# The spectral stage's B product over 128 array lines, with Y turned by transfers inside SBUF, and one order of units over all batches

## The chip, the cores and the metric

The kernel runs on one core of a Trainium2 chip. The core has TensorE (PE, matrix products into PSUM), VectorE (DVE), ScalarE (ACT), GpSimd (POOL) and SyncE (SP, which here issues transfers only). The metric is device microseconds of one execution; lower is better. The time before is 894.48 us, the median of three runs (893.96 to 896.12).

## The reference

The input x has 8 batches of 3008 rows by 256 columns. Along the rows it goes through a real Fourier transform, is multiplied by a complex 256 x 256 weight, gets a bias, is soft-thresholded at 0.01, and is transformed back. Every row of the result goes through a two-layer network with 2048 hidden units and an ELU.

```python
X = np.fft.rfft(x, axis=1)
Yr = Xr @ w_r - Xi @ w_i + b_r
Yi = Xr @ w_i + Xi @ w_r + b_i
Yr = np.sign(Yr) * np.maximum(np.abs(Yr) - lam, 0.0)      # Yi likewise, lam = 0.01
y = np.fft.irfft(Yr + 1j * Yi, n=3008, axis=1)
h = y @ w_in                                              # 256 -> 2048
g = np.where(h > 0.0, h, np.exp(np.minimum(h, 0.0)) - 1.0)
out = g @ w_out                                           # 2048 -> 256
```

## The kernel before

**Two stages in one stream.** 3008 = 47 x 64, so each Fourier transform is done as two short ones with a re-sorting through DRAM between them. A batch's spectral work is cut into 40 *units* that PE computes: 6 units A (first short transform, 2 matmuls each), 8 units X (second short transform, 8 matmuls), 12 units M (the complex weight, by three products, 6 matmuls), 6 units B (first inverse transform, 8 matmuls) and 8 units Y (second inverse transform, 8 matmuls). After the A units the result A is stored to a DRAM tensor DA and read back re-sorted as Z; after the B units, Bz is stored to DB and read back as Bs. Y units give yT, the input of the network, in bf16.

The network runs over blocks of 512 rows; batches do not end on block borders. Each block has 8 *steps*, 376 steps in all (47 per batch). A step i does, in PE's order: two front matmul groups (L797, one per hidden slice of 128), with at most one spectral unit between them, and then the back matmuls of step i - 2 (L852, 8 matmuls in fp32r). ACT takes exponentials of the front result, POOL or DVE clamps them, DVE mixes them into gT (L832), which the back matmuls read two steps later. After the last of a block's eight steps the output is copied from PSUM to osb, one half by DVE and one by ACT (L863), and stored by SP (L870); this falls on the steps with i mod 8 = 1, called output steps below.

**What a unit costs the other engines.** Each unit's PSUM result (one tile, pool psF) is evicted before the next unit may write it: by ACT for A, X, B and Y (L126, L336). An M step is different (`unit_M`, L244): DVE adds the product K and the bias (L272, L273, or L266 and L269 where DVE adds the whole bias), POOL adds the rest of the bias (L282), clips (L283) and subtracts (L286), which gives Y; POOL also makes the difference Xd for the M unit two further on (L240). In a step without M, POOL clamps the exponentials (L820, two of 128x512); in a step with M, ACT does a variant that needs no clamp (L811, L813). The POOL work of an M is queued in `jobs` and its last part is issued in the step after.

**The B unit** (`unit_B`, L311). Y holds two M units' results (i = 0, 1); its 128 partitions are two halves (s = 0, 1) of 64, and its columns hold real and imaginary part (c = 0, 1). The inverse product sums over 64 lines and over c, so before the change it has eight matmuls of 64 lines by 256 columns, two of which accumulate into each of four results. M3 is the table of sines and cosines for it.

**The order of units** (`plan(b)`, L879) is written per batch of 47 steps: Y units of batch b, the 8 X, 12 M and 6 B of batch b + 1 with A units of batch b + 2 as filler between, then the first two Y of batch b + 1 so that they fall on steps 38 + b and 39 + b of the 47. `f0` holds the unit of a step, `f1` what is issued after it: loads of x (POOL's queue), of Z and Bs (SP's queue), the first differences. With A for a filler, Y for a Y unit and "-" for no unit, the order before (47 steps to a line, from step 0) is

```
-YY-YYXXXXXXXXYMMMMBMYMBMMBMMBMMBABAAAYYAA-----
YYXXXXXXXXYMYMMYMBMYMBMMBMAMBMMBABAAAA-YY------
YYXXXXXXXXYMYMMYMBMYMBMAMBMAMBMMBABAAA--YY-----
YYXXXXXXXXYMYMMYMBMYMBMAMBMAMBMAMBABAA---YY----
YYXXXXXXXXYMYMYMYMBMAMBMAMBMAMBMAMBABA----YY---
YYXXXXXXXXYMYMYMYMBMAMBMAMBMAMBMAMBABA-----YY--
YYXXXXXXXXYMYMYMYMBM-MBM-MBM-MBM-MB-B-------YY-
YYYYYY-----------------------------------------
```

Batch 0's units up to its second Y, and batch 1's A units, are done ahead of step 0, in the first 58 us.

Of the kernel before, what the change touches and what calls it, by code (L numbers as in the profile page):

```python
# [16 lines left out]
N2 = 64  # L17
K1 = 24
# [7 lines left out]
def kernel(  # L26
# [31 lines left out]
    wcat_s = constp.tile([P, 2, 2 * D], BF16, name="wcat_s")  # L58
# [5 lines left out]
    bias_p = constp.tile([P, 2 * D], BF16, name="bias_p")  # L64
# [16 lines left out]
    xtp = ctx.enter_context(tc.tile_pool(name="xtp", bufs=1))  # L81

# [20 lines left out]
    Bz_of = {}  # L103
    DB_of = {}
# [97 lines left out]
    def m_group(b, q, i, ps, biased=False):  # L202
        XT = XT_of[b]
        o = (2 * q + i) * P
        if biased:
            nc.tensor.matmul(ps, lhsT=busy[:, 0:P], rhs=bias_p[:], start=True, stop=False)
# [25 lines left out]
    jobs = []  # L232

# [10 lines left out]
    def unit_M(b, q, i):  # L244
# [15 lines left out]
        Y_ = Y_of[b, q]  # L260

        def done():
            two = lambda t: t.rearrange("p (c d) -> p c d", c=2)
            if b == 1 and k % 2 == 0:
                Kb = wk1.tile([P, 2 * D], F32, name="Kb", tag="Kb")
                nc.vector.tensor_tensor(  # L266
                    two(Kb[:]), kp.unsqueeze(1).to_broadcast([P, 2, D]), two(bias_bc[:]), ALU.add
                )
                nc.vector.tensor_tensor(yb[:], ps[:, 0], Kb[:], ALU.add)  # L269
# [3 lines left out]
            nc.vector.tensor_tensor(  # L273
                two(yb[:]), two(ps[:, 0]), Kb.unsqueeze(1).to_broadcast([P, 2, D]), ALU.add
            )
# [3 lines left out]
        def clip_():  # L279
            clips.append(wk2.tile([P, 2 * D], F32, name="clip", tag="clip"))  # L280
            if not (b == 1 and k % 2 == 0):
                nc.gpsimd.tensor_tensor(yb[:, D : 2 * D], yb[:, D : 2 * D], bias_d[:], ALU.add)  # L282
            nc.gpsimd.tensor_scalar(clips[0][:], yb[:], LAM, -LAM, ALU.min, ALU.max)  # L283

        def sub_():
            nc.gpsimd.tensor_tensor(Y_[:, i, :], yb[:], clips[0][:], ALU.subtract)  # L286

        jobs.append((clip_, lambda: unit_D(b, k + 2), sub_))
        later(False, done)

# [20 lines left out]
    def unit_B(b, v, alone=False, on_dve=False):  # L311
# [5 lines left out]
        Bz, Y = Bz_of[b, v // 2], Y_of.pop((b, v))  # L317
        ps = unit_ps("bps", alone)
        for pp in range(2):
            for c in range(2):  # L320
                for s in range(2):
                    nc.tensor.matmul(  # L322
                        ps[:, s, pp * D : pp * D + D],
                        lhsT=M3[s * N2 : s * N2 + N2, 2 * v + pp, c, :],
                        rhs=Y[s * N2 : s * N2 + N2, pp, c * D : c * D + D],
                        start=(c == 0), stop=(c == 1),
                    )
        def done():
# [3 lines left out]
            if on_dve:  # L332
                nc.scalar.copy(Bv[:, :, 0], psv[:, :, 0])
                nc.vector.tensor_copy(Bv[:, :, 1], psv[:, :, 1])
            else:
                nc.scalar.copy(Bv, psv)  # L336
# [35 lines left out]
    busy = constp.tile([P, 512], BF16, name="busy")  # L372
    nc.vector.memset(busy[:], 1.0)
    ips = pre0.tile([P, 512], F32, name="ips", tag="pre0")

    def idle_pe(n):

        for _ in range(n):
            nc.tensor.matmul(ips[:], lhsT=busy[:, 0:P], rhs=busy[:], start=True, stop=True)
# [295 lines left out]

    def fB(v, on_dve=False):
# [10 lines left out]
    nc.scalar.copy(bias_p[:], brow[:])  # L687
    nc.vector.tensor_tensor(rest[:], brow[:], bias_p[:], ALU.subtract)
    for u in range(8):
# [7 lines left out]
        idle_pe(1)  # L697
    for o, src, sc, bi in ((1, w3, TURN, 0.0), (0, a3, -TURN, hpi[:])):
        nc.scalar.activation(
            M3[:, :, 0, o * N2 : o * N2 + N2], src[:], AF.Sin, bias=bi, scale=sc  # L700
# [3 lines left out]
        M3[:, :, 1, 0:N2], M3[:, :, 0, N2:P], 2.0, sgb, ALU.mult, ALU.mult  # L704
# [3 lines left out]
        M3[:, :, 1, N2:P], M3[:, :, 0, 0:N2], -2.0, sgb, ALU.mult, ALU.mult  # L708
# [170 lines left out]
    def plan(b):  # L879

        f0 = [[] for _ in range(PER)]
        f1 = [[] for _ in range(PER)]
        n1, n2 = b + 1, b + 2
        lead = int(b == 0)
        early = 6 if b == 0 else 4
        seq = [("y", u) for u in range(2, early)]
        if b == 0:
            seq.insert(2, ("-",))
        rest_ = []
        if n1 < B:  # L890
            due = 38 + b
            seq += [("X", u) for u in range(8)]
            fill = [("y", u) for u in range(early, 8)]
            if n2 < B:
                fill += [("A", u) for u in range(6)]
            else:
                fill += [("-",)] * 6
            room = max(0, min(9, due - 5 - (b > 0) - lead - len(seq) - 17))
            fill, rest_ = fill[:room], fill[room:]
            cut = ([-1, 4] if b == 0 else [-1, 11, 0, 4, 8, 2, 6, 10, 1, 11])[: len(fill)]  # L900
            fill = fill[::-1]
            seq += [fill.pop() for c in cut if c < 0]
            for k in range(12):
                seq.append(("M", k // 2, k % 2))
                if k % 2 and k > 1:
                    seq.append(("B", k // 2 - 1))
                for c in cut:
                    if c == k:
                        seq.append(fill.pop())
            if b == 0:  # L910
                seq.append(rest_.pop(0))
            seq.append(("B", 5))
            k = due - lead - len(seq)
            seq += rest_[:k] + [("-",)] * (k - len(rest_))
            seq += [("n", 0), ("n", 1)] + rest_[k:]
        else:
            seq += [("y", u) for u in range(early, 8)]
        xs = (14, 18, 22) if b == 0 else (1, 4, 7)
        for t, u in enumerate(seq, lead):
            if u[0] == "y":  # L920
                f0[t].append(put("Y", b, u[1]))
            elif u[0] == "n":
                f0[t].append(put("Y", n1, u[1]))
            elif u[0] == "A":
                if n2 < B:
                    f0[t].append(put("A", n2, u[1]))
            elif u[0] == "M":
                f0[t].append((unit_M, (n1, *u[1:])))
            elif u[0] != "-":
                f0[t].append(put(u[0], n1, *u[1:]))  # L930
            if u == ("X", 7):
                for k in range(2):
                    f1[t + 1].append((unit_D, (n1, k)))
            if u == ("B", 5):
                f1[t + (0 if b == 0 else 1)] += [(load_Bs, (n1, w)) for w in range(4)]
            if u == ("A", 5) and n2 < B:
                f1[t] += [(load_Z, (n2, s0, s1)) for s0, s1 in ((0, 8), (8, NS))]
        if b == 0:
            f1[5].append((weight_sum, (0,)))
            f1[6].append((weight_sum, (1,)))  # L940
            f1[7].append((weight_sum, (2,)))
            f1[4].append((scale_w_in, (3, True, 0)))
            f1[4].append((scale_w_in, (3, True, 1)))
        if n2 < B:
            for ci in range(3):
                f1[xs[ci]].append((load_x, (n2, ci)))
        return f0, f1

    f0 = f1 = None
    was = None  # L950
    kinds = []

    for i in range(n + LAG):
        split = False
        if i < n:
            r = i % PER
            if r == 0:
                f0, f1 = plan(i // PER)
                used = [bool(u0 or u1) for u0, u1 in zip(f0, f1)]
                kinds = ["M" if any(f is unit_M for f, a in f0[k]) else "F" for k in range(PER)]  # L960
            kind = kinds[r]
            then = kinds[r + 1] if r + 1 < PER else "F"
# [5 lines left out]
            for f, a in f0[r]:  # L968
# [11 lines left out]
            for f, a in f1[r]:  # L980
# [56 lines left out]
```

## Time and profile before

| What | Value |
|---|---|
| median of three runs | 894.48 us |
| profiled execution, its own time | 893.78 us |
| its span, first to last instruction | 892.0 us |
| step 0 begins, step 375 begins | 58.0 us, 882.8 us |
| mean granted TensorE clock | 0.998 |
| B matmuls (L322) | 384 of 64x256, mean 272 ns, 29.4 us busy |
| transfers on SP's and ACT's queues | 77.62 MB, 30.9% of the 16 DMA engines |

"Busy" of PE is the union of its instructions' times; matmuls overlap, so 48 matmuls of 0.27 us each do not take 48 x 0.27. The length of a step, from the start of its first L797 matmul to that of the next step, is the better measure, and the views below are read that way.

### The profile page before, as it was taken

The numbers are of one execution on the slowest core, as the hardware profiler recorded it, in microseconds if no ns is written. First come the engines' busy times: TensorE is split into PE (matmuls) and PEld (weight loads), VectorE is DVE, ScalarE is ACT, GpSimd is POOL, SyncE is SP. The second block draws the span as 40 slices with busy tenths as digits, with TensorE's granted clock in tenths as the row PEclk, the third lists the DMA queues.
The fourth block names the chain that finished last, engine by engine and source line by source line (L and its number), as shares of the span: only waits on it lengthen the run. The fifth ranks groups of instructions, "written<-read, shape, count | busy, mean of one in ns | idle before, by whom it ended". The sixth has DMA issues, their size and how long they took to land.

```text
span 892.0 us, 18350 instructions
## 1 busy us (share of the span) xinstructions
PE 875.0 (98%) x6889; PEld 665.5 (75%) x6889; DVE 656.0 (74%) x1066; ACT 708.6 (79%) x1132; POOL 659.6 (74%) x990
## 2 busy tenths in 40 slices
PE   8889999999999999999999999999999999999997
PEld 3447776887778777887779877788777877778776
DVE  8766885777766777668876677767776677777775
ACT  6668888788887888788887888878887887777664
POOL 6707995679856898669876799767986589866664
PEclk9999999999999999999999999999999999999999
DMA  8993435721285113850248312672227211141111
GB/s 255 351 271 80 126 112 166 213 95 49 71 229 167 55 48 104 227 167 24 72 119 237 119 28 88 165 218 85 68 88 187 63 36 48 58 120 38 31 42 48
DMA packets 90677, 106.32 MB, mean 119 GB/s; under 512 B 5270, under 2 KB 81308, under 8 KB 87228
## 3 DMA queue, kind: packets, MB, share of 16 engines
q1 hardware_dynamic: 84332, 77.62, 30.9%
q0 software_dynamic: 5968, 27.26, 9.8%
q8 instruction: 54, 0.88, 0.4%
q14 instruction: 35, 0.29, 0.1%
q10 hardware_dynamic: 288, 0.26, 0.1%
HBM read 55.32 MB, written 49.81 MB: 118 GB/s over the span
## 4 chain that ended last, share of the span: by engine, by line
PE 90%; DMA 4%; POOL 2%; ACT 1%; issue 1%; DVE 1%; SPq 0%; ACTq 0%; POOLq 0%
PE ps_o L852 38%; PE hps L797 36%; PE mps L256 6%; PE bps L322 3%; PE xps L192 2%; PE yps L363 2%; PE aps L158 2%; DMA DA<-A 1%; PE mps L209 1%; DMA Z<-DA 1%; DMA xt<-in_x_dram 1%; DMA Bs<-DB 0%; POOL Y L286 0%; ACT Et L811 0%; POOL xt L115 0%
## 5 line engine op out<-in xcount | busy, mean ns | idle before, releaser
L832 DVE SCALAR_TENSOR_TENSOR gT<-Et,hps 128x512 fp32r<-128x512 f32 x752 | 495.8, 683 | 170.0 <-POOL Et L820 142.9
L820 POOL TENSOR_SCALAR Et<-Et 128x512 f32<-128x512 f32 x576 | 350.1, 615 | 190.1 <-ACT Et L815 188.1
L852 PE MATMUL ps_o<-w_out_r,gT 128*128 128x256 f32 x3008 | 476.8, 301 | 0.9 <-ACT osb L863 0.5
L852 PEld LDWEIGHTS ps_o<-w_out_r,gT 128*128 128x128 f32 x3008 | 403.3, 189 | 53.2 <-ACT osb L863 5.3
L797 PE MATMUL hps<-yT,w_in_s 128*128 128x512 bf16 (+4 forms) x1728 | 438.1, 354 | 1.4 <-DVE gT L832 0.6
L815 ACT ACTIVATE Et<-hps 128x512 f32<-128x512 f32 x584 | 341.4, 603 | 95.4 <-PE hps L797 92.8
L797 PEld LDWEIGHTS <-w_in_s 128*128 128x128 bf16 x1728 | 118.4, 98 | 57.6 <-issue 22.1
L811 ACT ACTIVATE Et<-hps 128x512 f32<-128x512 f32 x168 | 100.7, 599 | 52.8 <-PE hps L797 51.3
L286 POOL TENSOR_TENSOR Y<-yb,clip 128x512 bf16<-128x512 f32 x84 | 108.3, 1290 | 0.3
L813 ACT ACTIVATE Et<-Et 128x1024 f32<-128x1024 f32 x84 | 88.9, 1058 | 2.7
L282 POOL TENSOR_TENSOR yb<-yb,bias_d 128x256 f32<-128x256 f32 x78 | 57.1, 732 | 13.5 <-DVE yb L273 12.3
L283 POOL TENSOR_SCALAR clip<-yb 128x512 f32<-128x512 f32 x84 | 51.5, 613 | 9.4 <-DVE yb L269 2.5
L272 DVE TENSOR_TENSOR Kb<-mps,bias_bc 128x256 f32<-128x256 f32 x78 | 33.0, 423 | 34.4 <-PE mps L256 34.2
L240 POOL TENSOR_TENSOR Xd<-XT 128x256 bf16<-128x256 bf16 x84 | 56.1, 672 | 0.0
L273 DVE TENSOR_TENSOR yb<-mps,Kb 128x512 f32<-128x512 f32 x78 | 53.9, 691 | 2.7
L126 ACT CAST yT<-yps 128x752 bf16<-128x752 f32 x63 | 49.2, 781 | 3.4 <-PE yps L363 3.4
L126 ACT CAST A<-aps 128x1024 bf16<-128x1024 f32 x45 | 45.5, 1011 | 7.6 <-PE aps L158 6.7
L126 ACT CAST XT<-xps 128x768 bf16<-128x768 f32 x61 | 48.4, 795 | 3.2 <-PE xps L192 3.2
L256 PE MATMUL mps<-wsum,XT 128*128 128x256 bf16 x336 | 50.4, 273 | 0.0
L336 ACT CAST Bz<-bps 128x1024 bf16<-128x1024 f32 x46 | 46.3, 1007 | 0.4 <-PE bps L322 0.4
L192 PEld LDWEIGHTS <-Z 96*128 96x128 bf16 x512 | 28.7, 98 | 15.9 <-DMA Z<-DA 3.4
L363 PEld LDWEIGHTS <-Bs 96*128 96x128 bf16 x512 | 28.1, 98 | 16.4 <-DMA Bs<-DB 3.9
(118 smaller groups left out, 489.0 us busy)
## 6 DMA issues: line engine op xcount, KB each, us to landing
xt<-in_x_dram POOLq DMA_DIRECT2D x21, 1024.0 KB, 5.6
out_dram<-osb SPq DMA_DIRECT2D x158, 128.0 KB
Bs<-DB SPq DMA_DIRECT2D x32, 384.0 KB
DA<-A SPq DMA_DIRECT2D x21, 512.0 KB
DB<-Bz SPq DMA_DIRECT2D x21, 512.0 KB
Z<-DA SPq DMA_DIRECT2D x7, 1152.0 KB
Z<-DA SPq DMA_DIRECT2D x11, 384.0 KB
xt<-in_x_dram POOLq DMA_DIRECT2D x6, 512.0 KB, 6.0
```

The lines of the kernel that those rows point to most:

```text
L126: nc.scalar.copy(dst, src)
L240: nc.gpsimd.tensor_tensor(Xd_of[b, k][:], XT[:, :, 0, o : o + P], XT[:, :, 1, o : o + P], ALU.subtract)
L256: nc.tensor.matmul(dst, lhsT=lhs(dt), rhs=rhs(dt), start=dt == 0, stop=dt == 1)
L282: nc.gpsimd.tensor_tensor(yb[:, D : 2 * D], yb[:, D : 2 * D], bias_d[:], ALU.add)
L286: nc.gpsimd.tensor_tensor(Y_[:, i, :], yb[:], clips[0][:], ALU.subtract)
L797: nc.tensor.matmul(hps[s][:, c0:c1], lhsT=w_in_s[:, dt, ft * P : ft * P + P], rhs=yT_of[b][:, dt, t0 : t0 + c1 - c0], start=(dt == 0), sto ...
L811: nc.scalar.activation(e, h, AF.Relu, scale=-1.0)
L813: nc.scalar.activation(self.E, self.E, AF.Exp, scale=-1.0)
L815: nc.scalar.activation(e, h, AF.Exp)
L820: nc.gpsimd.tensor_scalar(e, e, 1.0, 0.0, ALU.min, ALU.max)
L832: nc.vector.scalar_tensor_tensor(g_of[self.i][:, p], self.E[:, p], -1.0, self.h[p], ALU.add, ALU.max)
L852: nc.tensor.matmul(po[q][:, i_ % 2, :], lhsT=gT[:, s, i_ * P : i_ * P + P], rhs=w_out_r[:, ft, :], start=(ft == 0 and i_ % 2 == 0), stop=( ...
```

## The change

It has two parts. (1) For batches 2 to 7, Y is laid out [partition, c, i, column], and after POOL has subtracted for the second of two M units, `turn_Y` issues four transfers from SBUF to SBUF on SP's queue. Each moves 64 partitions by 1 KB, and together they make Yt, in which the 128 partitions are (c, 64 lines) and s is in the columns. `unit_B` then has four matmuls of 128 lines by 256 columns, each with its own 128 x 128 table. That table M3 is turned once, by four transfers in steps 24 and 25 (`turn_M3`), from M3f, which lies in a buffer of yT that is free until then; batches 0 and 1 use M3f with the old eight matmuls. ACT's eviction of the new B result is one contiguous copy. Yt has two buffers; until batch 2 they hold the weights wcat_s and, in `spare`, bias_p and the operand of the idle matmuls.

(2) `plan(b)` is replaced by `units()`, which goes through the steps and picks at most one unit by rules (whose inputs are ready, what is due), and `plan()`, which hangs loads and differences onto the chosen steps. B of batches 2 to 7 comes at least 6 steps after the second M of its pair (3 for batch 1), the first Y units mostly 7 steps after the last B, M is kept off the output steps unless M is late, and Z of batches 3 to 7 is loaded in four parts. Where an M is followed at once by another, DVE adds its whole bias (`whole`). The order after, 47 steps to a line, is

```
-YY-YYXXXXXXXXYMMMMBMBMMMBMBMMYMBABAAAYYAAYYYYY
XXXXXXXXAMMAMMAMBMMBMMMBMMBABAYB-A----YYXXXXXXX
XAMAMAMYYMBAMAMYYMBAMBMMYMBMYB---B-XXXXYYXXXXAM
AMAMAMAMYYMBBMAMYYMBYMBMYM-B---B----XXYYXXXXXXA
MYYMAAMAMBMAMAMBMYYMBYMBMYM-B---B----XXYYXXXXXX
AMYYMAAMAMBMAMAMBMYYMBYMBMYM-B---B----XXYYXXXXX
XYMYMYMYMYMBMYMBM-MBM-MBM-B---B------YYYYYYYY--
-----------------------------------------------
```

The core of the diff:

```diff
-    M3 = constp.tile([P, K1 // 2, 2, P], BF16, name="M3")
+    M3 = constp.tile([P, K1, P], BF16, name="M3")
...
-            Y_of[b, q] = wk3.tile([P, 2, 2 * D], BF16, name="Y", tag="Y")
+            Y_of[b, q] = wk3.tile([P, 2, 2, D], BF16, name="Y", tag="Y")
+        Y_ = Y_of[b, q][:, i] if b == 1 else Y_of[b, q][:, :, i]
...
-            if b == 1 and k % 2 == 0:
+            if (b, k) in whole:
...
-            nc.gpsimd.tensor_tensor(Y_[:, i, :], yb[:], clips[0][:], ALU.subtract)
+            two = lambda t: t[:].rearrange("p (c d) -> p c d", c=2)
+            nc.gpsimd.tensor_tensor(Y_, two(yb), two(clips[0]), ALU.subtract)
+            if b > 1 and i == 1:
+                turn_Y(b, q)
...
+    def turn_Y(b, q):
+        Y = Y_of.pop((b, q))
+        Yt_of[b, q] = wk2.tile([P, 2, 2 * D], BF16, name="Yt", tag="Yt")
+        for s in range(2):
+            for c in range(2):
+                nc.sync.dma_start(
+                    Yt_of[b, q][c * N2 : c * N2 + N2, s],
+                    Y[s * N2 : s * N2 + N2, c].rearrange("p i d -> p (i d)"),
+                )
...
+            Yt = Yt_of.pop((b, v))
+            for j in range(4):
+                nc.tensor.matmul(
+                    psj[:, j], lhsT=M3[:, 4 * v + j],
+                    rhs=Yt[:, j % 2, j // 2 * D : j // 2 * D + D], start=True, stop=True,
+                )
...
+                nc.scalar.copy(Bz[:, o : o + 4, :], psj)
...
+    def turn_M3(c):
+        for h in range(2):
+            nc.sync.dma_start(
+                M3[c * N2 : c * N2 + N2].rearrange("p (j h) m -> p j h m", h=2)[:, :, h],
+                M3f[c][h * N2 : h * N2 + N2],
+            )
...
+    LB, YB, ZX, LEAD = 6, 7, 6, 54
+    def units():
...
+                if kind == "X":
+                    ok = t >= 6 if b == 1 else (
+                        t >= when("A", b, 5) + ZX and t > when("M", b - 1, 11)
+                        and t >= due(b, 0) - LEAD
+                    )
+                elif kind == "M":
+                    ok = t >= when("X", b, 7) + 2
+                elif kind == "B":
+                    ok = t >= when("M", b, 2 * k + 1) + lag
...
+            if t == 3:
+                u = None
+            elif must:
+                u = must
+            elif "M" in can and was != "M" and (tight or t % NPAIR != 1):
+                u = can["M"]
+            elif "B" in can:
+                u = can["B"]
+            elif "M" in can and tight:
+                u = can["M"]
+            else:
+                early = t < 6 or ("y" in can and can["y"][2] < 2)
+                u = next((can[k] for k in ("yXA" if early else "XAy") if k in can), None)
...
+            if kind == "M" and k < 11 and (
+                k % 2 == 0 if b == 1 else at[kind, b, k + 1] == t + 1
+            ):
+                whole.add((b, k))
...
+            if (kind, k) == ("A", 5):
+                for p in range(2 if b == 2 else 4):
+                    w = 8 if p == 0 or b > 2 else 24
+                    f1[t + (0, 1, 3)[min(max(b - 2, 0), 2)] * p].append((load_Z, (b, 8 * p, 8 * p + w)))
```

More of the change, by code (lines that the diff above doesn't have):

```diff
@@ L205, in m_group @@
         if biased:
-            nc.tensor.matmul(ps, lhsT=busy[:, 0:P], rhs=bias_p[:], start=True, stop=False)
+            nc.tensor.matmul(ps, lhsT=busy[:, 0:P], rhs=bias_p, start=True, stop=False)
         for m, (c, wm) in enumerate(((0, wcat_r), (1, wcat_s))):
@@ L232 @@
     jobs = []
+    whole = set()
     def unit_D(b, k):
@@ L378, in idle_pe @@
         for _ in range(n):
-            nc.tensor.matmul(ips[:], lhsT=busy[:, 0:P], rhs=busy[:], start=True, stop=True)
+            nc.tensor.matmul(ips[:], lhsT=busy[:, 0:P], rhs=busy, start=True, stop=True)
     brow, rest = (wk3.tile([P, 2 * D], F32, name="yb", tag="yb") for _ in range(2))
@@ L697 @@
         idle_pe(1)
+    M3t = late2.tile([P, 2, S], BF16, name="M3f", tag="yT")
+    M3f = [
+        M3t[:, c, 0 : K1 // 2 * P].rearrange("p (j m) -> p j m", m=P) for c in range(2)
+    ]
     for o, src, sc, bi in ((1, w3, TURN, 0.0), (0, a3, -TURN, hpi[:])):
         nc.scalar.activation(
-            M3[:, :, 0, o * N2 : o * N2 + N2], src[:], AF.Sin, bias=bi, scale=sc
+            M3f[0][:, :, o * N2 : o * N2 + N2], src[:], AF.Sin, bias=bi, scale=sc
         )
@@ new lines, with due @@
+    LB, YB, ZX, LEAD = 6, 7, 6, 54
+    def due(b, w):
+        return (S * b + S // 4 * w) // TB * NPAIR - 1
+    def units():
+        at = {("A", 1, k): 0 for k in range(6)} | {("y", 0, k): 0 for k in range(2)}
+        xat = {(2, c): s for c, s in enumerate((14, 18, 22))}
+        xat |= {(3, c): PER + 1 + 3 * c for c in range(3)}
+        when = lambda *u: at.get(u, 10 * n)
+        many = {"X": 8, "M": 12, "B": 6, "A": 6, "y": 8}
+        count = lambda kind, b: sum((kind, b, k) in at for k in range(12))
+        was = None
+        for t in range(1, n):
+            can, must = {}, None
+            for kind, m in many.items():
+                b = next((b for b in range(B) if (kind, b, m - 1) not in at
+                          and (b or kind == "y") and (kind != "A" or b > 1)), None)
+                if b is None:
+                    continue
+                k = count(kind, b)
+                lag, wait = (3, 4) if b == 1 else (LB, YB)
+                if kind == "X":
+                    ok = t >= 6 if b == 1 else (
+                        t >= when("A", b, 5) + ZX and t > when("M", b - 1, 11)
+                        and t >= due(b, 0) - LEAD
+                    )
+                elif kind == "M":
+                    ok = t >= when("X", b, 7) + 2
+                elif kind == "B":
+                    ok = t >= when("M", b, 2 * k + 1) + lag
+                elif kind == "A":
+                    ok = (
+                        t >= xat[b, k // 2] + 6 and t > when("X", b - 1, 7)
+                        and (k < 5 or count("M", b - 1) < 10 or t > when("B", b - 1, 5) + 1)
+                    )
+                else:
+                    ok = (t > 3 or k < 4) if b == 0 else t >= when("B", b, 5) + wait + (k > 1)
+                    if t >= due(b, k // 2) - 2 + k % 2 + (b == 1 and k < 2):
+                        must = kind, b, k
+                if ok:
+                    can[kind] = kind, b, k
+            tight = False
+            if "M" in can:
+                _, b, k = can["M"]
+                lag, wait = (3, 4) if b == 1 else (LB, YB)
+                tight = t + 11 - k + min(6 - count("B", b), (13 - k) // 2) >= due(b, 0) - 1 - wait - lag
+            if t == 3:
[8 more added lines that the diff above has]
+                u = can["M"]
+            else:
+                early = t < 6 or ("y" in can and can["y"][2] < 2)
+                u = next((can[k] for k in ("yXA" if early else "XAy") if k in can), None)
+            was = u and u[0]
+            if u:
+                at[u] = t
+                if u[0] == "A" and u[2] % 2 and 2 < u[1] + 1 < B:
+                    xat.setdefault((u[1] + 1, u[2] // 2), t + 4)
+        return at, xat
@@ new lines, in plan @@
+    def plan():
+        f0 = [[] for _ in range(n + PER)]
+        f1 = [[] for _ in range(n + PER)]
+        at, xat = units()
+        for (kind, b, k), t in at.items():
+            if kind == "M" and k < 11 and (
+                k % 2 == 0 if b == 1 else at[kind, b, k + 1] == t + 1
+            ):
+                whole.add((b, k))
+        for (kind, b, k), t in at.items():
+            if t == 0:
+                continue
+            name = "Y" if kind == "y" else kind
+            f0[t].append(put(name, b, *((k // 2, k % 2) if kind == "M" else (k,))))
+            if (kind, k) == ("X", 7):
+                f1[t + 1] += [(unit_D, (b, j)) for j in range(2)]
+            if (kind, k) == ("B", 5):
+                f1[t + (b > 1)] += [(load_Bs, (b, w)) for w in range(4)]
+            if (kind, k) == ("A", 5):
+                for p in range(2 if b == 2 else 4):
+                    w = 8 if p == 0 or b > 2 else 24
+                    f1[t + (0, 1, 3)[min(max(b - 2, 0), 2)] * p].append((load_Z, (b, 8 * p, 8 * p + w)))
+        for (b, c), t in xat.items():
+            f1[t].append((load_x, (b, c)))
+        for k in range(3):
+            f1[5 + k].append((weight_sum, (k,)))
+        for c in range(2):
+            f1[24 + c].append((turn_M3, (c,)))
+            f1[4].append((scale_w_in, (3, True, c)))
@@ L947, in plan @@
         return f0, f1
-    f0 = f1 = None
+    f0, f1 = plan()
+    kinds = ["M" if any(f is unit_M for f, a in u) else "F" for u in f0]
     was = None
-    kinds = []
     for i in range(n + LAG):
@@ L955 @@
         if i < n:
[L956 to L962, printed above, removed]
+            kind, then = kinds[i], kinds[i + 1]
             split = i > LAG and (i - LAG) % NPAIR == NPAIR - 1
@@ L967 @@
             front_mm(i, h, 0)
[L968 removed]
+            for f, a in f0[i]:
                 f(*a)
@@ L979 @@
                 was.mix()
-            for f, a in f1[r]:
+            for f, a in f1[i]:
                 f(*a)
```

115 lines of the change are left out of this document (28 added, 87 removed).

## The prediction

> **What bounds the kernel now.** I read the page's busy shares and chain first, then the PE timeline step by step, then the tables by stretch, then the groups of POOL and ACT, the waits, and SP's queue.
>
> ```profile
> PE 875.0 (98%) x6889; PEld 665.5 (75%) x6889; DVE 656.0 (74%) x1066; ACT 708.6 (79%) x1132; POOL 659.6 (74%) x990
> PE 90%; DMA 4%; POOL 2%; ACT 1%; issue 1%; DVE 1%; SPq 0%; ACTq 0%; POOLq 0%
> ```
>
> PE is on the chain for 90% of the span. So the time is a sum of PE steps, one per front pair of the second stage, and each step's length can be read from the first L797 matmul of one step to that of the next. The table by stretch for four such steps (a B unit, an M unit, an A unit, no unit), and one step with no unit right after an output step:
>
> ```profile
> core 0: us, PE busy (x) PEld busy (x) DVE busy (x) ACT busy (x) POOL busy (x), PEclk, DMA share, GB/s
> 309.43:311.91 2.48, 2.48 (x23) 1.63 (x21) 1.85 (x3) 2.48 (x4) 2.39 (x4) 1.00 0.00 0
> 311.91:314.37 2.46, 2.46 (x20) 1.98 (x19) 1.82 (x4) 1.65 (x4) 2.46 (x4) 1.00 0.00 0
> 323.93:326.22 2.29, 2.29 (x16) 1.69 (x15) 1.88 (x4) 2.29 (x4) 2.12 (x4) 1.00 0.09 27
> 359.94:361.74 1.80, 1.80 (x14) 1.38 (x13) 1.05 (x2) 1.44 (x3) 1.09 (x2) 1.00 1.03 244
> 767.33:769.86 2.53, 2.25 (x14) 1.32 (x13) 2.37 (x4) 2.41 (x4) 1.86 (x3) 1.00 0.07 20
> ```
>
> The first number after the stretch is its length. Nearly all steps of one kind have one length: 1.80 empty, 2.14 Y, 2.15 X, 2.29 A, 2.467 M, 2.475 B, at full clock. From step 3 (63.24 us) to the last (882.81) 819.6 us pass; the steps' kinds, each at its usual length, sum to 812.6. The other 7.0 us are stalls: 2.9 in steps 16 to 41 (batch 1's stages), 4.1 later. The PE timeline of a B and an M unit:
>
> ```profile
> 309.43 0.61 PE L797 MATMUL hps<-yT,w_in_s 128*128 128x512 bf16 x2
> 309.96 0.61 PE L322 MATMUL bps<-Y,M 64*128 64x256 bf16 x8
> 310.51 0.60 PE L797 MATMUL hps<-yT,w_in_s 128*128 128x512 bf16 x2
> ...
> 312.35 0.38 PE L256 MATMUL mps<-wcat_r,Xd 128*128 128x256 bf16 x2
> 312.57 0.60 PE L256 MATMUL mps<-wsum,XT 128*128 128x256 bf16 x4
> 313.00 0.59 PE L797 MATMUL hps<-yT,w_in_s 128*128 128x512 bf16 x2
> ```
>
> Columns: start, length, row. M's six matmuls start 0.109 apart. B's eight start in pairs 4 ns apart (309.965 and 309.969, 310.085 and 310.089, then 310.194 and 310.304): the halves s=0 and s=1 already run at once, so eight cost four places. B pays elsewhere: its first matmul starts 0.53 after the step's start where M's unit starts at 0.44, and the next L797 starts 0.205 after its last pair where 0.109 is usual. Two gaps of about 0.1 us, entering and leaving the 64-row form.
>
> **Part 1: four 128-row matmuls for eight of 64 rows, 36 times (batches 2 to 7).** The new B matmul has M's very form (128*128, 128x256). M adds 2.467 - 1.80 = 0.667 for six, 0.111 each; four add 0.445, and a B step takes 2.245 instead of 2.475: 0.23 x 36 = 8.3 us, all on PE, hence on the path. The lower bound is the A step: ACT does the same in both (two exponentials of 0.603, an eviction of 1.007 for B, 1.011 for A: 2.22 us), and A's take 2.29 without a stall; should ACT set B's step there, 0.18 x 36 = 6.5. I take 8.3, since PE's rows set M's and A's steps alike.
>
> The Trainium skill speaks against this part: "TensorE: Matmul & The Clock Gate" (Part 3) says that matmuls on different row groups run concurrently, so halving their number alone would save nothing; the pairs 4 ns apart agree. "TensorEngine Tiling (Array Packing)", Key Properties, says that a change of tiling mode drains the engine; the two 0.1 us gaps agree. By the first alone the sum loses all 8.3 us; by both it stands.
>
> **Part 2: the turn of Y.** Per pair of M units, four transfers of 64 KB go on SP's queue once POOL's second subtraction ends. In the trace that subtraction (L286) ends 7.1 to 7.3 us after its M step's start (8.7 at most; 4.8 to 6.8 if an M follows). B comes 6 steps after the second M in 20 pairs, 7 to 10 in 16. Six steps are 13.2 to 14.5 us by the lengths above, but 11.9 to 12.3 for the last pair of batches 3 to 7 (M11 at step 306, B at 312: one M, one B, four empty); B's matmuls start 0.44 later. Four issues cost 0.36 to 0.59 each, 1.9 in all. That leaves 4.5 us for the last to land, 3.0 for the tightest five.
>
> ```profile
> 15.42 3.23 DMA DA<-A
> 48.99 3.21 DMA DB<-A
> 145.00 8.13 DMA DA<-A
> ...
> 356.07 2.27 SPq L352 DMA_DIRECT2D Bs<-DB  x4
> ```
>
> These are transfers on the chain and SP's issue of four. A DRAM store of 256 KB took 3.2 us; 512 KB with three others in flight 8.1. A 64 KB transfer inside SBUF is nearest to the first: I take under 3.2, so no wait; the bound above is 8.1. Queued behind the waiting issue on SP stand output stores (two osb tiles, 8 steps apart), DA and DB stores, and Z and Bs loads. Only the last DB store and Bs loads are urgent: in batch 1 Y's first matmuls waited for Bs until 147.47, 11.0 us after B5's step began (136.51); the new order gives Y six to seven steps, 12.6 us or more, from batch 2 on. The first Z load of a batch blocks SP until DA has landed (6.9 us at most); it is issued at A5, and where turns follow (batches 4 to 7) their subtractions end no earlier. Yt's two tiles: each turn needs the B two pairs back, which runs at the latest one step after the new pair's last M, before its subtraction ends. All this at 0. M3's own turn (four transfers of 196 KB, steps 24 and 25) and ten more Z issues cost SP some 6 us over the span and no engine.
>
> **Part 3: the order.** Unit counts stay (84 M, 42 B, 36 A, 56 X, 62 Y, 96 empty), so only stalls change. Of the 4.1 us after step 41, about 3.0 come from M at an output step (i mod 8 = 1): ACT and DVE then also copy osb, and the next step waits.
>
> ```profile
> 767.33 1.22 PE L797 MATMUL hps<-yT,w_in_s 128*128 128x512 bf16 x4
> 768.81 1.21 PE L852 MATMUL ps_o<-w_out_r,gT 128*128 128x256 f32 x8 [0.25 <-ACT osb L863]
> ```
>
> Steps 66, 106, 202 and 298 (Y, 0.39 each) and 306 and 314 (empty, 0.73) pay. M stands there at twelve steps now, at four after (17, 57, 65, 121). I leave 0.64 for the last three. The rest is POOL, at these prices:
>
> ```profile
> L820 POOL TENSOR_SCALAR Et<-Et 128x512 f32<-128x512 f32 x576 | 350.1, 615 | 190.1 <-ACT Et L815 188.1
> L286 POOL TENSOR_TENSOR Y<-yb,clip 128x512 bf16<-128x512 f32 x84 | 108.3, 1290 | 0.3
> L282 POOL TENSOR_TENSOR yb<-yb,bias_d 128x256 f32<-128x256 f32 x78 | 57.1, 732 | 13.5 <-DVE yb L273 12.3
> L283 POOL TENSOR_SCALAR clip<-yb 128x512 f32<-128x512 f32 x84 | 51.5, 613 | 9.4 <-DVE yb L269 2.5
> L240 POOL TENSOR_TENSOR Xd<-XT 128x256 bf16<-128x256 bf16 x84 | 56.1, 672 | 0.0
> ```
>
> An M costs POOL 3.31 us (2.58 when DVE adds the bias, now also for seven M of batches 2 and 3: 0.73 off POOL, 0.26 onto DVE), another step 1.23. Batch 2 becomes denser, 12 M in 17 steps: 6 x 3.31 + 6 x 2.58 + 5 x 1.23 = 41.5 us of POOL against 40.9 of PE (before, 12 in 20 steps: 49.5 against 48.7, at 0.5 of POOL stalls). Batches 3 to 6 thin out, M and others in turn: 4.54 of POOL against at least 4.6 of PE. Batch 7 keeps M-empty pairs, 0.18 each. I put 1.3 there: 1.9 later stalls in place of 4.1, so 2.2 less; bounds 4.1, and -1.5 if runs of three M stall like step 16 (0.66). Batch 1 keeps 8-matmul B and nearly its order: its 2.9 stay.
>
> **Sum.** 8.3 + 2.2 = 10.5 us off the profiled execution's 893.78 (span 892.0): 883.3. The median of the runs, 894.48, stands 0.7 above that execution, so 884.0.
>
> **Rivals.** (a) ACT sets the B step and no stall goes: 6.5 off, 888.0. For: ACT is busy 2.48 of 2.48 in the B stretch; against: its work sums to 2.22. (b) The two gaps are issue time and stay (the profile names no other releaser): only 2.2 off, 892.3. Against: M, A and X units have none. (c) The slower side: turns land late. It decides on one number, the landing of a 64 KB transfer: from about 5.0 us the 20 six-step pairs lose half a microsecond each and the gain is gone; at 6 us, 20 x 1.5 = 30 us of PE waits, 914. For: the 8.1 us row; against: the 3.2 us rows and a DMA share near 0 through most M stretches.
>
> **How the numbers follow.** Forecast 0.71, (a) 0.13, (b) 0.05, (c) 0.11. A measurement of this kernel tells 0.3% (2.7 us) from no change: (b) is the "same", (c) the "slower", the others "faster". The forecast's own range is 880 (2.9 of early and all later stalls gone) to 887; with (a) 879.5 to 890 holds a little over 0.8.
>
> **What would show it.** B steps of batch 2 on at 2.245, matmuls 0.109 apart, no gap on either side (2.29: (a); 2.475: (b)). No wait of PE for a transfer into Yt; any such wait over 10 us in sum is (c). PE waits for osb from 5.3 us to under 2; steps 16 to 41 as they are. The prediction is wrong if PE waits for Yt, or if POOL's lag in batch 2 costs several microseconds.

## The result, and the profile after

The changed kernel takes 900.25 us (median of 8 runs, 897.81 to 902.98) against 894.99 us (8 runs, 893.81 to 896.45) before: a ratio of 1.006, with a 95% interval of 1.0042 to 1.0077. It is slower by 0.6%; 884.0 had been forecast, and 900.25 lies outside the range of 879.5 to 890.0. The profiled execution took 900.36 us, with a span of 898.4. Its busy shares and its chain, from the page:

```profile
PE 871.4 (97%) x6745; PEld 672.6 (75%) x6745; DVE 657.4 (73%) x1066; ACT 709.1 (79%) x1132; POOL 653.4 (73%) x983
PE 78%; DMA 7%; POOL 7%; DVE 3%; ACT 2%; issue 2%; SPq 1%; POOLq 0%; DVEq 0%; ACTq 0%
```

PE is 3.6 us less busy than before, so the matmuls did get cheaper. But PE's share of the chain fell from 90% to 78%, while DMA's rose from 4% to 7% and POOL's from 2% to 7%: PE now waits for others. Where, the table by stretch shows, here for five steps: a B unit of batch 2, a step with no unit, the first X of batch 3 (step 87), and two later B units (steps 120 and 208).

```profile
core 0: us, PE busy (x) PEld busy (x) DVE busy (x) ACT busy (x) POOL busy (x), PEclk, DMA share, GB/s
240.22:242.47 2.25, 2.25 (x18) 1.78 (x16) 1.25 (x3) 1.89 (x4) 1.78 (x3) 1.00 0.66 179
246.58:248.38 1.80, 1.80 (x15) 1.39 (x13) 1.08 (x3) 1.45 (x3) 1.09 (x2) 1.00 0.82 248
258.06:268.81 10.75, 3.79 (x23) 2.84 (x21) 2.04 (x4) 2.27 (x4) 1.84 (x3) 0.75 0.82 264
344.14:347.99 3.85, 2.57 (x18) 1.70 (x17) 2.56 (x4) 2.60 (x4) 2.54 (x4) 1.00 0.66 158
541.92:546.32 4.40, 2.57 (x19) 1.70 (x17) 3.19 (x6) 2.60 (x4) 2.56 (x4) 1.00 1.06 291
```

The new B step is 2.25 us, as forecast (the median of the 36 is 2.257, against 2.480 before). Its PE rows:

```profile
240.22 0.61 PE L840 MATMUL hps<-yT,w_in_s 128*128 128x512 bf16 x2
240.66 0.60 PE L355 MATMUL bps<-Yt,M 128*128 128x256 bf16 x4
241.10 0.59 PE L840 MATMUL hps<-yT,w_in_s 128*128 128x512 bf16 x2
```

The unit starts 0.44 after the step, and the next front matmul 0.44 after the unit's first, which is four places of 0.11: both gaps of the old form are gone. One X step, usually 2.15, is 10.75 us, with a mean granted clock of 0.75 in it. The waits of the trace name what PE stood for (total, times, longest):

```profile
PE xps L196 <- DMA Z<-DA: 7.5, 3, 7.0
PE bps L355 <- DMA Yt<-Y: 3.0, 2, 1.8
PEld ps_o L895 <- ACT osb L906: 1.5, 3, 0.6
```

Before, Yt did not exist, and the other two were:

```profile
PEld ps_o L852 <- ACT osb L863: 5.3, 11, 0.7
PE xps L192 <- DMA Z<-DA: 1.6, 3, 1.2
```

The whole span can be set out like this: take the start of every step from 3 to 375 and compare each step's length with the usual one of its kind (the lengths of the prediction, and 2.245 for a new B). What is over is a stall. (Summed with the lengths just as the prediction prints them, the usual lengths come out 1.0 us lower and the late stalls 1.0 higher, in each column alike; the differences between the columns stay.)

| us, profiled execution | before | after | forecast |
|---|---|---|---|
| step 3 starts at | 63.2 | 62.3 | 63.2 |
| usual lengths, summed | 812.6 | 804.4 | 804.3 |
| stalls up to step 41 | 2.9 | 4.5 | 2.9 |
| stalls after step 41 | 4.0 | 17.6 | 1.9 |
| step 375 starts at | 882.8 | 888.8 | 872.3 |

The gain of 8.2 us is there: 0.22 us per B step by the medians. Stalls of 22.1 us, where 4.8 had been forecast (6.9 before), take it and more. Of the 17.6 late ones, 9.3 lie at steps 87 and 88 (X of batch 3), 3.8 at steps 120 and 208 (B), 1.5 at three more B steps of 0.5 each (104, 112, 152), and 3.0 in pieces of at most 0.4.

**Step 87.** SP's queue, POOL's loads of x, ACT's eviction of the last A and the X that waits (rows of the SP, POOL, ACT and PE timelines), and the two longest pieces of the chain there:

```profile
241.13 0.59 POOL L119 DMA_DIRECT2D xt<-in_x_dram  x1
242.39 0.37 SPq L377 DMA_DIRECT2D DB<-Bz  x1
245.43 1.01 ACT L130 CAST A<-aps 128x1024 bf16<-128x1024 f32 x1
249.29 1.74 SPq L385 DMA_DIRECT2D Bs<-DB  x4
251.12 0.38 SPq L176 DMA_DIRECT2D DA<-A  x1
252.63 0.59 POOL L119 DMA_DIRECT2D xt<-in_x_dram  x1
261.97 0.77 SPq L185 DMA_DIRECT2D Z<-DA  x2
265.62 0.82 PE L196 MATMUL xps<-M,Z 96*128 96x96 bf16 x8 [6.96 <-DMA Z<-DA]
```

```profile
251.12 10.84 DMA DA<-A
261.97 3.60 DMA Z<-DA
```

ACT has the last A of batch 3 out of PSUM at 246.44. Its store to DA starts only at 251.12: SP stands at the loads of Bs for batch 2, which wait until the store to DB has landed, 6.9 us after its issue, beside 1 MB of x that POOL asked for just before it. The DA store then runs beside 1.5 MB of Bs and a further 1 MB of x and takes 10.8 us; Z takes 3.6 more. The first X of batch 3 comes 7 steps after that last A (steps 80 and 87) and has 14.2 us from the A step's start; before, it came 12 steps after (84 and 96). PE waits 6.96 us. And that is not all the loss:

```profile
262.00:263.00 1.00, 0.00 (x0) 0.00 (x0) 0.00 (x0) 0.00 (x0) 0.00 (x0) 1.00 0.16 37
263.00:264.00 1.00, 0.00 (x0) 0.00 (x0) 0.00 (x0) 0.00 (x0) 0.00 (x0) 0.68 0.81 266
264.00:265.00 1.00, 0.00 (x0) 0.00 (x0) 0.00 (x0) 0.00 (x0) 0.00 (x0) 0.50 0.91 246
268.00:269.00 1.00, 1.00 (x7) 0.91 (x7) 0.34 (x1) 0.00 (x0) 0.61 (x1) 0.50 1.03 270
270.00:271.00 1.00, 1.00 (x14) 0.94 (x12) 0.00 (x0) 1.00 (x2) 0.40 (x1) 0.91 0.22 61
```

The figure after POOL's is the granted clock. It falls to 0.50 in the fifth microsecond of idleness and comes back after some 4.5 us of work. From the end of the wait to the start of step 88 pass 3.19 us in place of 1.71, and step 88 is 0.67 too long: 2.15 us on top of the wait. The fall and the return of the clock are what the Trainium skill states, "TensorE: Matmul & The Clock Gate" (Part 1): after an idle window of about 3.4 us the clock gate passes half the pulses, until a window has been busy. The trace agrees.

**Steps 120 and 208.** SP's queue ahead of the B of step 208, and the B itself:

```profile
528.05 0.36 SPq L176 DMA_DIRECT2D DA<-A  x1
532.44 0.34 SPq L185 DMA_DIRECT2D Z<-DA  x1
532.87 3.57 SPq L913 DMA_DIRECT2D out_dram<-osb  x5
536.56 2.58 SPq L305 DMA_DIRECT2D Yt<-Y  x4
544.27 0.85 PE L355 MATMUL bps<-Yt,M 128*128 128x256 bf16 x4 [1.75 <-DMA Yt<-Y]
```

POOL had finished the subtraction at 530.80. The turn could be issued 5.8 us later only, since SP stood at the Z load, which waited for DA, and then issued five output stores that had queued up behind it. Then the landing was slow as well: B's second matmul, the first to need the last two transfers, starts at 544.62, 5.5 us after the end of the last issue, with a load of Z and 1 MB of x running beside. PE waited 1.75 us, although this B stands eight steps behind its M and not six. At step 120 the wait is 1.24, and the shares differ: the turn was issued only 1.1 us after the subtraction (338.11, after 337.01), and the landing took 5.6 us, again beside a load of Z and 1 MB of x. A late issue alone need not cost anything: of the 36 turns 27 were issued within 0.1 us of the subtraction, and the latest of all, 6.3 us after it (644.94, after 638.63, for step 256), landed within 3.2 us of its last issue's end and PE did not wait. What stands around it on SP is as at step 208, a Z load ahead and one beside, but no x is being loaded there.

### The profile page after: what moved, and what is told of

It reads as the page before. It is cut to its first block, busy times and chain, and to the rows that moved or that the text cites. A ratio compares the mean times of both kernels' runs of the same rounds, so it can differ in the third digit from the quotient of the medians.

```text
span 898.4 us, 18339 instructions
## 1 busy us (share of the span) xinstructions
PE 871.4 (97%) x6745; PEld 672.6 (75%) x6745; DVE 657.4 (73%) x1066; ACT 709.1 (79%) x1132; POOL 653.4 (73%) x983
## 4 chain that ended last, share of the span: by engine, by line
PE 78%; DMA 7%; POOL 7%; DVE 3%; ACT 2%; issue 2%; SPq 1%; POOLq 0%; DVEq 0%; ACTq 0%
PE ps_o L895 32%; PE hps L840 31%; PE mps L261 5%; DMA DA<-A 3%; PE xps L196 2%; POOL Y L292 2%; DMA Z<-DA 2%; POOL Et L863 2%; PE aps L162 2%; PE yps L396 2%; PE bps L355 2%; PE mps L213 1%; DMA Yt<-Y 1%; POOL yb L287 1%; POOL clip L288 1%
## 5 line engine op out<-in xcount | busy, mean ns | idle before, releaser
L840 PEld LDWEIGHTS <-w_in_s 128*128 128x128 bf16 x1728 | 121.5, 98 | 54.6 <-issue 15.5
L287 POOL TENSOR_TENSOR yb<-yb,bias_d 128x256 f32<-128x256 f32 x71 | 52.0, 732 | 29.4 <-DVE yb L278 28.4
L278 DVE TENSOR_TENSOR yb<-mps,Kb 128x512 f32<-128x512 f32 x71 | 49.1, 691 | 2.6
L277 DVE TENSOR_TENSOR Kb<-mps,bias_bc 128x256 f32<-128x256 f32 x71 | 29.9, 421 | 21.8 <-PE mps L261 21.0
L196 PE MATMUL xps<-M,Z 96*128 96x96 bf16 x512 | 32.9, 208 | 9.6 <-DMA Z<-DA 7.5
```

What stands on the lines that cost most here:

```text
L196: nc.tensor.matmul(psv[:, kk, 0 : 4 * K1], lhsT=Z[:, k, dt * P : dt * P + P], rhs=M2[:, k].rearrange("p c m -> p (c m)"), start=True, stop ...
L840: nc.tensor.matmul(hps[s][:, c0:c1], lhsT=w_in_s[:, dt, ft * P : ft * P + P], rhs=yT_of[b][:, dt, t0 : t0 + c1 - c0], start=(dt == 0), sto ...
```

## The experiments

The theory after reading the traces: (T1) the new order asks for batch 3's X before its data can be there, since x, DB, Bs, DA and Z share the DMA engines and SP's queue in the same 20 us; the turn itself costs little, and the 128-line B is worth its 8.2 us. The rivals: the transfers of the turn delay the other transfers, or the new B, not the order, is what costs.

**1. More room for batch 3's X.** X of batch 3 from 12 steps after the last A, as in the order before, not 6.

```diff
-                        t >= when("A", b, 5) + ZX and t > when("M", b - 1, 11)
+                        t >= when("A", b, 5) + (12 if b == 3 else ZX) and t > when("M", b - 1, 11)
```

> Edit: batch 3's X units start no earlier than 12 steps after its last A unit (step 92 in place of 87), the rest of the order by the same rules. Theory 1 (the new order asks for batch 3's Z too early: PE waits 7.1 us at step 87 and then runs some 2 us longer at half clock): the 9.3 us there go, about 891, 888 to 893. Theory 2 (the 144 turning transfers keep the DMA queue full, so Z is late wherever it is asked for): the wait stays or moves, 897 or more.

Measured: 890.33 us (889.85 to 891.04), ratio to the kernel before 0.9953 (0.9937 to 0.9969). The stall at steps 87 and 88 is gone, and nothing of its size took its place: late stalls 6.7 in place of 17.6, with waits for Yt still at step 208 (2.1 us over) and now at 126 (0.75). T1 holds; 9.9 us by a number in one line of the order. The edit also moves the units behind X, though, so the next run leaves every unit where it is.

**2. The same step 87, but x of batch 4 later.** The second and third load of x for batch 4 at steps 88 and 92, not 78 and 84. The order of units stays.

```diff
-            f1[t].append((load_x, (b, c)))
+            f1[{(4, 1): 88, (4, 2): 92}.get((b, c), t)].append((load_x, (b, c)))
```

> Edit: the loads of x for batch 4, parts 1 and 2 (1 MB each), are issued at steps 88 and 92 in place of 78 and 84; the order of units is that of the change. Theory 1 with shared bandwidth (from 250 to 262 us Bs 1.5 MB, DA 0.5 MB and x 1 MB run together at some 270 GB/s, and Z waits for DA): 1 MB less ahead of DA is 3.9 us, so PE's wait at step 87 falls from 7.1 to about 3 and the half clock after it goes: about 895. Theory 2 (turning transfers fill the queue): no change, 900.

Measured: 893.42 us (890.38 to 894.95), ratio 0.9981 (0.9968 to 0.9994). SP's queue in this run:

```profile
245.53 0.37 SPq L377 DMA_DIRECT2D DB<-Bz  x1
248.73 1.74 SPq L385 DMA_DIRECT2D Bs<-DB  x4
250.56 0.38 SPq L176 DMA_DIRECT2D DA<-A  x1
258.65 0.77 SPq L185 DMA_DIRECT2D Z<-DA  x2
```

The DB store lands in 3.2 us in place of 6.9, DA in 8.1 in place of 10.8, and step 87 is 0.97 over in place of 8.6. So two loads that no one needed yet made most of the stall: the lateness comes from sharing, and the order's 7 steps would nearly do without it.

**3. No turn.** The four transfers are left out, and B's four matmuls read Y as it lies (so the regrouping of Y is not computed); everything else is as in the changed kernel.

```diff
-            if b > 1 and i == 1:
-                turn_Y(b, q)
...
-            Yt = Yt_of.pop((b, v))
+            Yt = Y_of.pop((b, v))[:].rearrange("p c i d -> p c (i d)")
```

> Edit: the four turning transfers of each pair of M units are left out, and B's four matmuls of 128 lines read Y itself, so the part that regroups Y by real and imaginary part is not computed; order and PE work are those of the change. Theory 1: the waits for Yt at steps 120 and 208 go (3.75 us), the wait for Z at step 87 stays, since no turn is in flight in the 10 us before it: about 896.5. Theory 2: the wait for Z goes too, 888 or less.

Measured: 898.19 us (897.70 to 899.30), ratio 1.0042 (1.0025 to 1.0058). The chain at step 87 has the same two pieces:

```profile
252.77 11.41 DMA DA<-A
264.20 3.91 DMA Z<-DA
```

Without any transfer of the turn, DA takes 11.4 us and step 87 is 8.85 over. The turn is not what makes DA late. The waits of steps 120 and 208 are gone (step 208 keeps 0.56, which is not the transfer's). By the medians all 144 transfers together cost some 2 us of the 900, by the waits in the trace 3.0; the intervals of the two ratios overlap, so the times alone do not tell it from nothing.

**4. The order alone.** The new order with the eight 64-line matmuls and no turn.

```diff
-        if b < 2:
+        if True:
...
-            if b > 1 and i == 1:
-                turn_Y(b, q)
```

> Edit: the new order of units, with the eight 64-line matmuls of before for all batches and no turning of Y or M3. Theory 1: 36 B units cost 0.23 us more each (8.2), the waits for Yt go (3.75), the wait for Z stays: about 904.5. Theory 2 (the transfers make Z late): 895. If the order itself were no worse than before: 894.

Measured: 903.02 us (901.70 to 903.60), ratio 1.0096 (1.0077 to 1.0115): the order by itself makes the kernel slower, by 8.6 us, and step 87 is 7.3 over in it. Less that stall it would take 895.7 (an estimate from these two numbers) against 894.45 before, so the rest of the order gains nothing either. Its 36 B steps have the median of before again, 2.480, against 2.257 with the new B under the same order.

**5. The new B alone.** Four matmuls and the turn, with the steps taken from the `plan(b)` of before.

```diff
...
-    f0, f1 = plan()
+    whole |= {(1, k) for k in range(0, 12, 2)}
+    f0, f1 = ([u for p in (plan(b) for b in range(B)) for u in p[h]] + [[]] * PER for h in range(2))
```

> Edit: the order of units of before (B comes 3 to 5 steps after the second M of its pair), with the four 128-line matmuls and the turning transfers for batches 2 to 7. The subtraction ends 7.2 us after that M begins and four issues take 1.9, so by the step lengths the 36 B units wait 29 us in all if the last transfer lands 2 us after its issue, 46 us at 3.2, 109 us at 5 (the landing seen at step 120). Theory 1 (the six-step lag is what the transfers need; landings of 3 to 5 us in company): 932 to 990, every last B of a batch waiting longest. Rival (transfers land in time even at the old lag, so the new order was not needed for them): 887.

Measured: 928.43 us (927.51 to 930.06), ratio 1.0374 (1.0352 to 1.0396). There the B comes 3 to 5 steps after the second M of its pair, too early for the turn. The waits, and the last B of batch 7 on SP and PE, and the clock behind it:

```profile
PE bps L355 <- DMA Yt<-Y: 27.1, 18, 2.9
```

```profile
806.73 2.42 SPq L305 DMA_DIRECT2D Yt<-Y  x4
809.40 0.27 PE L355 MATMUL bps<-Yt,M 128*128 128x256 bf16 x1 [2.79 <-DMA Yt<-Y]
810.64 0.50 PE L355 MATMUL bps<-Yt,M 128*128 128x256 bf16 x3 [0.97 <-DMA Yt<-Y]
```

```profile
812.00:814.00 2.00, 2.00 (x8) 1.13 (x8) 0.58 (x1) 0.82 (x3) 0.61 (x1) 0.50 0.39 124
```

This is the clean measure of the turn. The second matmul of B is the first to need the last two transfers; it starts 1.5 us after the end of the fourth issue (810.64 less 809.15). With 2.4 us of issues, Yt is ready 3.9 us after the subtraction where nothing else is in flight. At steps 120 and 208 of the changed kernel the same matmul starts 5.6 and 5.5 us after the last issue's end. Of the 44 us of stalls that this run has over the kernel before, 32 lie at the six last B of a batch, which stand three steps behind the last M: 4.5 to 6.7 each, PE's wait and the half clock after it. Of the 24 pairs with five steps, 21 lose at most 0.3 us. So neither part is faster alone: the new B needs an order that leaves it more than three steps (the runs do not show that six are needed), and the order alone, by run 4, gains nothing.

**6. Z loads of batches 4 to 7 three steps later.** This takes SP's stand at the Z load, and the load itself, out of the way of the turns behind it.

```diff
-                    f1[t + (0, 1, 3)[min(max(b - 2, 0), 2)] * p].append((load_Z, (b, 8 * p, 8 * p + w)))
+                    f1[t + (3 if b > 3 else 0) + (0, 1, 3)[min(max(b - 2, 0), 2)] * p].append((load_Z, (b, 8 * p, 8 * p + w)))
```

> Edit: the loads of Z for batches 4 to 7 are issued three steps later, all else as in the change. Theory 1 (at steps 120 and 208 the turn stood on SP's queue behind a Z load that waited for DA, and output stores behind that, and then shared the queue with Z): the waits for Yt fall from 3.75 to under 1, step 87 stays, about 897. Rival (a turn's landing takes 5 us by itself): 900 and the same waits.

Measured: 898.33 us (895.05 to 901.57), ratio 1.0039 (1.0024 to 1.0054); by the medians 1.9 us below the changed kernel, with overlapping intervals, so the trace has to decide. SP's queue at the place of step 208:

```profile
526.45 0.36 SPq L176 DMA_DIRECT2D DA<-A  x1
526.98 4.04 SPq L913 DMA_DIRECT2D out_dram<-osb  x5
531.14 2.43 SPq L305 DMA_DIRECT2D Yt<-Y  x4
534.25 0.59 SPq L185 DMA_DIRECT2D Z<-DA  x1
```

The turn is now issued before the Z load. PE has no wait for Yt left in this trace; step 208 is 0.50 over in place of 2.15 and step 120 as usual. So moving the Z load is enough to end both waits. That takes out two things at once, its place ahead of the turn on SP and its bytes beside the turn's landing, and the run does not part them (step 256 of the changed kernel points at x as the third party, which no run moved away from step 208). At step 208 the earlier issue is enough by itself: from its end at 533.57 to B's second matmul at 541.24 there are 7.7 us. At step 120 there are only 5.2, less than the 5.6 of the changed kernel, so there the landing became shorter. The slow landing is no accident of one trace: at step 208 of runs 1 and 2, with the Z load in its old place, it took 6.7 and 6.3 us.

**7 and 8. The corrections together.** Run 7 has the edits of 1, 2 and 6. Run 8 has those of 2 and 6, and X of batch 3 from 8 steps after the last A.

> Edit: three edits together: batch 3's X from step 92 on, the two loads of x at steps 88 and 92, Z of batches 4 to 7 three steps later. Theory 1: the 890.3 of the first edit less the wait of 1.6 at step 208 and some of the 0.75 at step 126: 888. Rival (what is left is POOL's lag in the denser stretch of M units that the later X makes): 890.

> Edit: as the three edits together, but batch 3's X starts at step 88 (8 steps after its last A unit, not 12), so that its M units stand less densely. Theory 1: Z, with 1 MB of x out of its way, lands about when X asks for it (a wait of 1 us at most at step 88), 888. If X at step 88 still waits several us: 892.

Measured: 888.79 us (888.07 to 891.42), ratio 0.9938 (0.9919 to 0.9958), and 889.73 us (889.33 to 892.12), ratio 0.9945 (0.9924 to 0.9966). Both have no stall at the first X of batch 3 and no wait for Yt of over 1 us. Eight steps do as well as twelve once x is out of the way. Run 7 is faster than the kernel before by 0.6%. Late stalls are 5.4 us, though, where the prediction left 1.9 and the kernel before has 4.0. The mended order was not run with the old B.

**9. One of the small stalls.** In run 7 the B steps 152 and 208 are still 0.5 over. They stand behind "M, two Y, M". The trace of run 7 at steps 151 and 152:

```profile
403.50 1.27 POOL L292 TENSOR_TENSOR Y<-yb,clip 128x512 bf16<-128x512 f32 x1
404.75 1.18 POOL L863 TENSOR_SCALAR Et<-Et 128x512 f32<-128x512 f32 x2
405.39 0.69 DVE L875 SCALAR_TENSOR_TENSOR gT<-Et,hps 128x512 fp32r<-128x512 f32 x1 [1.13 <-POOL Et L863]
405.99 0.42 DVE L277 TENSOR_TENSOR Kb<-mps,bias_bc 128x256 f32<-128x256 f32 x1
407.19 0.61 PE L355 MATMUL bps<-Yt,M 128*128 128x256 bf16 x4 [0.21 <-DVE yb L278]
```

POOL's subtraction stands ahead of its clamps; DVE's mix waits 1.13 us for them; DVE's bias additions, which free the PSUM tile of the M, come after the mix; and the B waits for that tile. Edit: DVE adds the whole bias of the first M there too.

```diff
-                k % 2 == 0 if b == 1 else at[kind, b, k + 1] == t + 1
+                k % 2 == 0 if b == 1 else at[kind, b, k + 1] in (t + 1, t + 3)
```

> On top of the three corrections together (888.79 us): where an M is followed by two other units and the next M, DVE adds the whole bias of the first M, as it does already where an M follows at once. This takes POOL's 0.73 us addition (yb<-yb,bias_d) out of those steps and gives DVE 0.26 us more. Theory: the B step that stands behind such a pair (M Y Y M B, steps 152 and 208) is 0.5 us over its usual 2.245, because POOL's subtraction of 1.27 us stands ahead of its second clamp, DVE's mix waits for that clamp (1.13 us), and so the bias addition that frees the PSUM tile of the second M comes late. With POOL 0.73 us earlier these two steps lose their 0.5 us each: about 1 us in all, 887.8 us, and the B steps at 2.25 to 2.3. Rival: DVE's own queue sets the end of that chain (its bias additions are now longer): the B steps stay at 2.75 or grow, and the time stays at 888.8 or above.

Measured: 888.28 us (887.21 to 888.95); the kernel before had 895.99 beside it, ratio 0.9912 (0.9896 to 0.9929). The two B steps fall from 2.78 and 2.75 us to 2.42 and 2.38, as the theory says:

```profile
406.40:408.82 2.42, 2.42 (x18) 1.70 (x17) 2.42 (x5) 2.42 (x4) 1.51 (x3) 1.00 0.00 0
406.86 0.61 PE L355 MATMUL bps<-Yt,M 128*128 128x256 bf16 x4
```

But DVE's longer additions make ten other steps (149, 157, 189 and others) 0.1 longer, so that the late stalls are 5.2 us against 5.4: given back. The mechanism is shown; by the total, runs 7 and 9 can't be told apart.

## Why the prediction was wrong

- **Part 1 (8.3 us) was right**, in size and in cause. B steps of 2.257 by the median in the changed kernel as in runs 1 to 3 and 5 to 9, 2.480 before and with the old matmuls under the new order (run 4): 0.22 x 36 = 8.0 us, or 8.2 by the lengths used above. Rivals (a) and (b) are out: ACT does not set the step, and the two gaps went with the 64-row form, which agrees with the drain that the Trainium skill names ("TensorEngine Tiling (Array Packing)", Key Properties). Its price here is 0.22 us per unit for the pair of them.
- **Part 2 ("all this at 0") failed**, in a sentence that was too narrow: "Only the last DB store and Bs loads are urgent." I followed Bs to Y and the turn to B, and never the last A to the first X, through DA and Z. That chain had lost five of its twelve steps for batch 3. From rows of before it needed the eviction (2.2 us from the step's start), a DA store ("6.9 at most") and Z (3.6 here): 12.7 of the 14.2 us to be had (13.9 with the 8.13 of its own row for a DA store). That looks like enough; what it left out is that the order also put two loads of x and the loads of Bs on top of it: 4.7 us of SP standing at Bs and 3.9 more for the store. Cost: 9.3 us, shown by run 1 (all of it back) and run 2 (most of it back).
- **The turn's own price held only where nothing else was in flight.** "1.9" for four issues is 2.4 (the prediction's own row of four Bs issues has 2.27); "under 3.2" for the landing is 1.5 alone (run 5), but 5.5 and 5.6 at the two places where PE waited, beside loads of Z and x. The other step that failed here is the assumption that SP gets to the issue when POOL is done. I wrote that the subtractions behind the first Z load "end no earlier"; at 208 one ended at 530.80, 1.6 us before that load got through, with five output stores still between. Cost of both: 3.0 us of PE waits, gone in run 6. A wait of PE for Yt was one of the prediction's signs of being wrong; it came, but it is the smaller part of the loss.
- **Rival (c)**, turns that land late, was given 30 us of waits; 3.0 came, under the 10 us that I had set as its mark. Its condition, a landing from 5.0 us, was seen where PE waited, at 2 of the 36 pairs. The slower side came true by a mechanism that was not on the list. Its chance of 0.11 for "slower" was thus too low by one whole rival.
- **Part 3 was mis-sized.** The wait for osb fell from 5.3 to 1.5, as forecast. But the late stalls did not fall to 1.9: with no wait for Z or Yt of over 1 us left (run 7) 5.4 remain, more than the 4.0 of before, because of the B behind "M, two Y, M" (0.5 each, run 9) and some 0.2 to 0.75 in batch 3 and in batch 7's pairs. And the "2.9" of batch 1 became 3.2 to 5.8 from run to run, so "nearly its order" did not keep its stalls.
- **The sum.** Run 7 has what the forecast meant, with its mistake in Part 2 mended: 888.8 in place of 884.0. Its stalls, 9.7 in place of 4.8, are that difference.

Not settled: why the stalls of steps 5, 38 and 41 differ between profiles of orders that are alike there (step 5 by up to 1.7 us, 38 and 41 by 0.5 and 0.7). No run was made on it.

## What to carry to other kernels

When an order of work is changed, list every chain that leaves the core's memory and comes back (store, wait, load, use), count its steps before and after, and price it with what the new order puts on the same queue and the same DMA engines in that window, not with the store's time alone. A transfer that must be prompt should not be queued behind one that waits: here moving Z loads by three steps ended the waits for Yt, and moving two loads of x by ten and eight ended most of the wait for Z. Two parts that each make a kernel slower (by 0.96% and 3.7% here) can be faster together: 0.6% here, once three places in the order were mended.

## What the runs showed of the hardware

- A wait of 6.96 us cost more than its length: the granted clock fell to 0.50 in the fifth microsecond and stayed there for some 4.5 us of work, 2.15 us lost on top. Less idleness was enough in run 5: waits of 1.96 and 1.04 us with one matmul between (step 271) brought it too, to 0.61 on average from 699 to 700 us and 0.50 from 700 to 701. After the waits of 2.79 and 0.97 shown above it fell only when work had resumed: 1.00 up to 811 us, 0.93 from 811 to 812, then 0.50. Behind the single wait of 1.75 us at step 208 of the changed kernel it stayed at 1.00.
- A 512 KB store to DRAM landed in 3.2 us (DB, run 2) with x out of the way and in 6.9 beside a load of 1 MB; DA took 8.1 beside 1.5 MB of loads and 10.8 beside those and 1 MB more.
- A 64 KB transfer inside SBUF was usable 1.5 us after the end of its issue when alone (run 5), and 5.5 to 6.7 us after it beside loads of x and Z (step 208 of the changed kernel and of runs 1 and 2).
